# Two slices of the first projection inside the attention prologue: a fused attention and feed-forward kernel on one core, with sums ahead of exps and the fifth unit's loads moved

## The chip, the cores and the metric

The kernel runs on one core of one Trainium2 chip. Time is device time in microseconds (us) of that core, as the median of several runs; one more run is made under the hardware profiler, and from it come the profile page and the trace. TensorE (PE) multiplies matrices and writes to PSUM, VectorE (DVE) and ScalarE (ACT) read PSUM and compute element by element, GpSimd (POOL) computes on SBUF and issues the DMAs that convert types, and SyncE (SP) issues the other DMAs.

## What is computed

```python
q_n = q / (np.linalg.norm(q, axis=-1, keepdims=True) + 1e-06)
k_n = k / (np.linalg.norm(k, axis=-1, keepdims=True) + 1e-06)
scores = np.matmul(q_n, k_n.transpose(0, 1, 3, 2)) / tau
scores = scores - np.max(scores, axis=-1, keepdims=True)
attn = np.exp(scores)
attn = attn / (np.sum(attn, axis=-1, keepdims=True) + 1e-09)
attn_out = np.matmul(attn, v)               # (8, 12, 448, 64)
x = attn_out.transpose(0, 2, 1, 3).reshape(8 * 448, 12 * 64)
h = x @ w_in                                # 768 -> 2048
out = (h * np.cos(h)) @ w_out               # 2048 -> 768
```

There are 8 batches, 12 heads, 448 positions and a head size of 64; tau is 0.1. Inputs and the output are float32 in HBM. With normed q and k no score is large, so the kernel takes exps without subtracting the maximum.

## The kernel before, in words

**Units and pairs.** A unit is six heads of one batch (16 units, `u`); a pair is two heads (48 pairs, `g`, three in each unit, six in each batch). For each unit SP loads q and k as six DMAs of 224 KB (`load`, two for each pair) into `raw`, which has two buffers, so that unit 4 reuses unit 2's buffer pair by pair. POOL loads v and both weight matrices (W1 and W2 in four quarters each) and converts them to bf16.

**Norms.** `square` (ScalarE or POOL) squares q and k, `reduce` (VectorE) sums over the head, `rnorm` (ScalarE, an ln and an exp, marked ln and rn) makes the inverse root, and `scale` (mostly POOL) multiplies: the result is `qks`.

**Transposes.** For pairs 0 to 8 (`g < TD`) TensorE transposes `qks` into a PSUM bank and VectorE copies it to `qkT` (one of three buffers). From pair 9 on SP does it as a DMA transpose (L619, labels T9, T10 ...).

**Attention of a pair.** `scores` runs in four steps c = 0 to 3 (a half one and three full ones), in turn in the PSUM tiles SC1 and SC0; after each, ScalarE takes the exp into `PX` (L666). `attend` multiplies exps by v (marked AV, L690) and by ones for the sums (marked S, L712 or L698), both in the PSUM tile AV; two small opening stages (R, L683) come before. For a direct pair ScalarE then takes lnS and expS (L745, L747), the reciprocal of the sums as exp(-ln), and VectorE multiplies to `xT` (L751; in the first six pairs it reads AV itself, so AV becomes free only then). For the other pairs AV and sums are copied out, and `chain` sends the sums through a gather DMA, a reciprocal, a store to HBM and a broadcast DMA (gather, spread, bcast, all on SP), and POOL multiplies (L784). Unit 2's reciprocal is made on POOL (L770, L771).

**First projection (`m1`).** For each batch, 16 slices n of 128 columns of W1, two slices (n = 2gi and 2gi + 1) in one two-bank PSUM tile; each slice accumulates six matmuls over the six pairs' `xT` (L798, "M1"). ScalarE takes the cosine as a sine (L813), VectorE multiplies (L815) into `gT`. Sine and exp need different ScalarE tables, loaded ahead of and behind `m1` (L498). Before, `m1(0)` takes the tiles SC0, SC1 and AV in turn (`TURN`), and opens its first two gi early, without the last pair.

**Second product (`m2`).** The output is made in 28 tiles of 128 rows. Between other work (`m2_fill`) TensorE takes a tile in quarters of its array (L873, four 64x64 pieces for each of 16 steps y and two halves h) into the banks PO and TP. It is held by the quarter of W2 (`y // 4`) and the slice of `gT` (`y // 2`) that a step reads. Before, tile 0 goes through y = 0 to 15 with h = 0, then with h = 1.

**Order.** All operations go into a `Program` that plays them with written-out costs: on ScalarE, VectorE, POOL and SP the ready operation with the earliest due time (`late`, moved by `bias`) goes next; on TensorE the prologue is chosen from a window of the program's order (`P.free`), and from `P.free = False` on the order is the program's. In TensorE's planned gaps in the prologue `emit` puts filler matmuls of zeros into PO. What an engine does is then fixed; only semaphores set the time. The prologue (L1026 to L1054) is: pairs 0 to 5, the loads of unit 2 and unit 3, weights, the last `attend`, `transposes(6)`, `m1(0)`, and the loads of unit 4 (L1054), which wait for nothing but the buffer. Then come pairs 6 to 47; inside pair 6 the transposes of pairs 7 and 8 stand (L1009 to L1011), the one in TP, the other in PO. `m1(1)` follows after pair 12's scores.

## Time and profile before

| | us |
|---|---|
| median of three runs | 437.56 |
| lowest, highest | 437.56, 440.69 |
| the profiled run | 438.43 |
| its span | 436.6 |
| ScalarE busy | 271.2 |
| POOL busy | 231.0 |

A line of a timeline has the start, the length, the engine, the line of the source, the operation, out <- in, the shape and the count of instructions in the row, and in brackets the idle time of the engine before it with what ended it. A line of the waits has who waited, for whom, the sum in us, how often, and the longest. "DMA to landing" is the smallest, median and largest time from issue to landing of the DMAs that a view chose. The chain is the work that ended last, followed back from the end; its rows have a start, a length and what. TensorE's granted clock is 1.00 all through the profile before.

### The profile page before, as it was taken

How to read it: one execution, taken by the hardware profiler on the slowest of the kernel's cores; microseconds unless marked ns; L12 is line 12 of the kernel's file. 1: busy time of each engine (PE TensorE's matmuls, PEld its weight loads, DVE VectorE, ACT ScalarE, POOL GpSimd, SP SyncE). 2: the span in 40 equal slices, each digit the busy share in tenths (PEclk: the TensorE clock that was granted, in tenths of full speed). 3: DMA queues.
4: the chain of work that ended last, by engine and by line, in shares of the span. 5: the costliest groups of instructions: out<-in, count | busy, mean ns of one | idle time of the engine just before them, and what ended most of it. 6: DMA issues, size and time to landing. Idle time of an engine off the chain costs nothing.

```text
span 436.6 us, 13537 instructions
## 1 busy us (share of the span) xinstructions
PE 419.8 (96%) x6056; PEld 231.5 (53%) x6056; DVE 188.0 (43%) x242; ACT 271.2 (62%) x356; POOL 231.0 (53%) x184
## 2 busy tenths in 40 slices
PE   8889989989999999999999999999999999999996
PEld 4334545545555555564556545665556545455563
DVE  3543762245742348331862158321862144323421
ACT  5987577775787745877478836776478845603400
POOL 4999927669755464744947095905947022003000
PEclk9999999999999999999999999999999999999999
DMA  8999997999669996649927997859956930151022
GB/s 190 250 257 220 245 206 107 164 208 204 125 83 112 214 207 168 137 105 203 238 46 157 181 217 139 137 107 216 235 102 101 149 98 2 40 137 38 2 72 72
DMA packets 80713, 64.32 MB, mean 147 GB/s; under 512 B 45712, under 2 KB 75408, under 8 KB 80656
## 3 DMA queue, kind: packets, MB, share of 16 engines
q1 hardware_dynamic: 62528, 50.68, 56.8%
q0 software_dynamic: 18048, 12.59, 19.5%
q8 instruction: 47, 0.77, 0.8%
q10 hardware_dynamic: 80, 0.20, 0.1%
q14 instruction: 10, 0.08, 0.1%
HBM read 55.67 MB, written 11.14 MB: 153 GB/s over the span
## 4 chain that ended last, share of the span: by engine, by line
PE 56%; DMA 15%; POOL 14%; issue 5%; ACT 3%; SPq 3%; DVE 2%; ACTq 0%; POOLq 0%; DVEq 0%
PE SC L798 16%; PE AV L798 9%; PE TP L873 7%; DMA W<-in_moe_w_out_dram 7%; PE PO L873 7%; POOL qks L602 4%; PE SC L651 4%; PE AV L690 4%; POOL xT L784 4%; POOL sq L570 3%; DMA sums<-xu 3%; DMA RB<-scr 3%; PE PO L903 2%; PE SC L903 2%; PE TP L903 2%
## 5 line engine op out<-in xcount | busy, mean ns | idle before, releaser
L666 ACT ACTIVATE PX<-SC 128x448 bf16<-128x448 f32 (+1 forms) x192 | 153.4, 823 | 27.5 <-PE SC L651 17.0
L873 PE MATMUL PO<-W,gT 64*64 64x384 bf16 x1408 | 143.4, 323 | 1.7 <-DVE qkT L640 0.9
L873 PE MATMUL TP<-W,gT 64*64 64x384 bf16 x1408 | 143.4, 324 | 0.4
L602 POOL TENSOR_TENSOR qks<-raw,rn 128x896 bf16<-128x896 f32 (+1 forms) x48 | 79.4, 1678 | 40.4 <-ACT rn L594 40.4
L798 PE MATMUL SC<-xT,W 128*128 128x448 bf16 x480 | 98.3, 353 | 0.0
L784 POOL TENSOR_TENSOR xT<-xu,RB 128x448 bf16<-128x448 f32 x37 | 41.0, 1136 | 100.7 <-DMA RB<-scr 100.7
L873 PEld LDWEIGHTS PO<-W,gT 64*64 64x64 bf16 x1408 | 76.4, 107 | 19.3 <-issue 3.3
L873 PEld LDWEIGHTS TP<-W,gT 64*64 64x64 bf16 x1408 | 76.1, 107 | 15.8 <-PE TP L873 2.2
L570 POOL TENSOR_TENSOR sq<-raw 128x896 bf16<-128x896 f32 x45 | 75.2, 1693 | 8.4 <-DMA raw<-in_q_dram 6.8
L813 ACT ACTIVATE cosb<-SC,cst 128x896 f32<-128x896 f32 x40 | 40.1, 1006 | 54.6 <-PE SC L798 53.3
L798 PEld LDWEIGHTS SC<-xT,W 128*128 128x128 bf16 x480 | 46.7, 98 | 44.1 <-POOL xT L784 0.4
L798 PE MATMUL AV<-xT,W 128*128 128x448 bf16 x288 | 62.0, 353 | 2.6 <-POOL xT L784 1.4
L577 DVE TENSOR_REDUCE n<-sq 128x14 f32<-128x896 bf16 (+2 forms) x49 | 51.5, 1055 | 6.8 <-ACT sq L568 5.7
L651 PE MATMUL SC<-qkT 64*64 64x448 bf16 x576 | 52.0, 359 | 1.5 <-ACT lnn L591 0.9
L815 DVE TENSOR_TENSOR gT<-SC,cosb 128x896 bf16<-128x896 f32 x40 | 43.5, 1089 | 22.0 <-ACT cosb L813 21.9
L813 ACT ACTIVATE cosb<-AV,cst 128x896 f32<-128x896 f32 x24 | 24.2, 1007 | 39.1 <-PE AV L798 39.1
L846 DVE COPY osb<-PO 128x384 f32<-128x384 f32 x26 | 14.5, 558 | 69.9 <-PE PO L873 63.4
L798 PEld LDWEIGHTS AV<-xT,W 128*128 128x128 bf16 x288 | 26.9, 98 | 32.1 <-POOL xT L784 5.0
L815 DVE TENSOR_TENSOR gT<-AV,cosb 128x896 bf16<-128x896 f32 x24 | 26.2, 1090 | 38.1 <-ACT cosb L813 38.0
L737 DVE COPY xu<-AV 128x896 f32<-128x896 f32 x23 | 25.0, 1086 | 40.5 <-PE AV L706 40.4
L690 PE MATMUL AV<-PX,va 128*32 128x448 bf16 x576 | 36.2, 356 | 0.0
L651 PEld LDWEIGHTS SC<-qkT 64*64 64x64 bf16 x576 | 16.2, 105 | 21.9 <-ACT PX L666 11.1
(66 smaller groups left out, 364.0 us busy)
## 6 DMA issues: line engine op xcount, KB each, us to landing
raw<-in_k_dram SPq DMA_DIRECT2D x48, 224.0 KB, 6.7
raw<-in_q_dram SPq DMA_DIRECT2D x48, 224.0 KB, 7.4
out_dram<-osb SPq DMA_DIRECT2D x55, 192.0 KB, 3.4
RB<-scr SPq DMA_DIRECT2D x22, 336.0 KB, 4.9
va<-in_v_dram POOLq DMA_DIRECT2D x32, 192.0 KB, 9.2
W<-in_moe_w_in_dram POOLq DMA_DIRECT2D x4, 768.0 KB, 15.0
W<-in_moe_w_out_dram POOLq DMA_DIRECT2D x4, 768.0 KB, 26.1
RB<-scr SPq DMA_DIRECT2D x4, 224.0 KB, 4.1
```

The costliest lines, as they stand in the source:

```text
L570: pool(lambda e, x=x, y=y: e.tensor_tensor(y, x, x, ALU.mult), src_, dst, 0.1 + n * 1.78e-3, label="sq%d.%d" % (u, p)).pad = LATE if u > 1 ...
L577: dve(lambda e, w=w: e.tensor_reduce(out=n2v[i][:, 2 * p : 2 * p + 2, w], in_=sqv[p][:, :, w, :], axis=mybir.AxisListType.X, op=ALU.add), ...
L602: f = lambda e, s0=s0, s1=s1: e.tensor_tensor(qksv[i][:, p, s0:s1].rearrange("p s h d -> p h s d"), rawv[i][:, h, s0:s1, :], bass.AP(rn[i] ...
L651: m = e.matmul(SCv[z][BP * o : BP * o + BP, a, 0:S], t[r, c - 1 + (NT3 + 1) * o, 0:BP], t[r, :, BP : 2 * BP], start=True, stop=True)
L666: act(lambda e: e.activation(PHv[j] if c == 0 else PXv[j][:, c - 1], SCv[z][:, :, 0:n], ACT.Exp, scale=1.0 / TAU), ["SC%d" % z], [("PX", j ...
L690: t = e.matmul(AVv[o : o + 32, 0, 0:S], vav[y][:, 2 * p + a, c + 1, d : d + 32], PXv[j][:, c, a, :], start=False, stop=(c == NT3 - 1))
L784: pool(lambda e, p=p: e.tensor_tensor(xTv[b % 2][:, UP * i + p, :], xuv[:, u % 3, p, :], RBv[i][:, p, :], ALU.mult), [("RB", i, p), ("xa", ...
L798: t = e.matmul(ph[:, a, 0:S], W1v[:, order[c], 128 * n : 128 * n + 128], xTv[b % 2][:, order[c], :], start=(c == 0), stop=(c == NKC - 1))
L813: act(lambda e, ph=ph, cz=cz: e.activation(cosv[cz], ph[:, :, 0:S], ACT.Sin, bias=cst.ap()[:, 0:1], scale=1.0), names(gi) + ["cst0"], [("c ...
L815: dve(lambda e, ph=ph, cz=cz, gi=gi: e.tensor_tensor(gTv[:, 2 * gi : 2 * gi + 2, S * (b % 2) : S * (b % 2) + S], ph[:, :, 0:S], cosv[cz], ...
L873: r = e.matmul(POH[b][x : x + 64, 0:HW], gTv[k, y, col + x : col + x + 64], W2v[k, y, HW * b : HW * b + HW], start=(y == 0 and h == 0), st ...
L903: r = e.matmul(po[:, 0:HW], gTv[:, y, col : col + 128], W2v[:, y, HW * hf : HW * hf + HW], start=(y == 0), stop=(y == NF - 1))
```

## The change

PO and TP become the two halves of one two-bank PSUM tile MP, so MP can hold two slices of the first projection. Its parts:

- The slices n = 0 and 1 of `m1(0)` accumulate the first four pairs' `xT` in MP right behind pair 5's last scores (`m1_step`, called in the prologue), then pair 4's and pair 5's. The order of tiles in `m1(0)` becomes MP, SC0, SC1, AV, twice (`first`), with three gi opened early. The number of matmuls is the same.
- The transposes of pairs 6, 7 and 8 stand inside `m1(0)`, at gi = 5, 6 and 7 (`inner`), all three in TP. Before, one stood ahead of it and two behind it.
- lnS and expS of the first six pairs are due 1.0 earlier (`bs`).
- Fillers stop at the last opening of the two slices, and after the first opening they add zeros without clearing the bank. The program has 50 in place of 61.
- Unit 4's loads of q and k wait until slice gi = 6 of `gT` is written (`u4`), which is inside `m1(0)`.
- Tile 0 of the second product goes through y = 0 to 7 for both halves, then y = 8 to 15 (`cut`).

What this does to the order on the engines: on TensorE nine matmuls of the first projection stand ahead of pair 5's last sum, before it was five; from the first matmul of the second product on, TensorE's order is the same. On ScalarE lnS and expS go ahead of the second half of the next pair's exps, and after `m1(0)` unit 3's ln comes behind five exps and its rn behind six (before, behind two), unit 4's much later. On VectorE the second copy of pair 0's transposes goes ahead of a reduction. On POOL a square and a W1 issue go ahead of the third scale, ahead of the sixth stand one square and one W1 issue more than before; after `m1(0)` unit 4's squares come between unit 3's second and third scale. On SP unit 4's loads stand just ahead of T9, unit 5's are split around T11, and the store of unit 2's reciprocals is followed by an output, T12 and the broadcast.

The diff, cut to its core:

```diff
     "late": 0.0,
     "mixed": (3, (0, 1, 2, 0, 1, 2, 0, 1), (2, 3, 4, 0, 1, 5)),
-    "other": 8,
-    "inside": 7,
+    "turned": 9,
+    "first": (3, 1, 2, 0, 3, 1, 2, 0),
+    "inner": 5,
+    "bs": -1.0,
+    "cut": 8,
+    "bx": 0.0,
...
+    "u4": (6,),
+    "v3": (),
...
+            opened = [o.start for o in self.ops if o.label == "M1 0.0"]
             for a, b in self.gaps:
                 t, a = a + room / 2, a + room
-                while a + took <= b:
-                    o = self.op("PE", fn, cost=took, mode="F", label="filler")
+                while a + took <= min(b, max(opened)):
+                    o = self.op("PE", lambda e, shut=t < min(opened): fn(e, shut), cost=took, mode="F", label="filler")
...
-    TPF = ps("TP", [128, 512], F32)
-    TP = TPF.bitcast(BF16)
-    AVT = AV.bitcast(BF16)
-    PO = ps("PO", [128, 512], F32)
-    POT = PO.bitcast(BF16)
+    MP = ps("MP", [128, 2 * 512], F32)
+    TPF, PO = MP.ap()[:, 0:512], MP.ap()[:, 512:1024]
+    TP, AVT = MP.bitcast(BF16).ap()[:, 0:1024], AV.bitcast(BF16).ap()
...
-        if g == PLAN["other"]:
-            bank, keys = [POT, POT], [["PO"], ["PO"]]
...
         act(lambda e: e.activation(xuv[:, 3 + i, p, :], AVv[:, 1, 0:S], ACT.Ln), ["AVs"], [("xs", i, p)], S, "E",
-            label="lnS%d" % g)
+            label="lnS%d" % g, bias=PLAN["bs"] if g < PB else 0.0)
         act(lambda e: e.activation(r, xuv[:, 3 + i, p, :], ACT.Exp, scale=-1.0), [("xs", i, p)], [("RB", i, p)], S, "E",
-            label="expS%d" % g)
+            label="expS%d" % g, bias=PLAN["bs"] if g < PB else 0.0)
...
+    BANKS = {"AV": ["AVa", "AVs"], "MP": ["TP", "PO"]}
+
+    def m1_step(b, bank, n, c0, c1, order):
+        a, (name, ph) = n % 2, PHs[bank]
+
+        def f(e):
+            for c in range(c0, c1):
+                t = e.matmul(ph[:, a, 0:S], W1v[:, order[c], 128 * n : 128 * n + 128], xTv[b % 2][:, order[c], :],
+                             start=(c == 0), stop=(c == NKC - 1))
+            return t
+
+        return P.op("PE", f, [("W1", n // 4)] + [("xT", b % 2, order[c]) for c in range(c0, c1)], BANKS.get(name, [name]),
+             cost=(c1 - c0) * MM, mode="F", label="M1 %d.%d" % (b, n))
+
+    def m1(b, early=0, split=NKC, turn=TURN, order=tuple(range(NKC)), done=0, inner={}):
...
+        for gi in range(done):
+            for a in range(2):
+                step(gi, a, NKC - 2, NKC - 1)
         for c0, c1 in [(0, split)] + [(c, c + 1) for c in range(split, NKC - 1)]:
-            for gi in range(early):
+            for gi in range(done, early):
                 for a in range(2):
                     step(gi, a, c0, c1)
         for gi in range(NF // 2):
+            if gi in inner:
+                transposes(inner[gi])
...
-        h, y0 = f // NF, f % NF
+        seg = [(h, y, w) for y, w in ([(0, PLAN["cut"]), (PLAN["cut"], NF - PLAN["cut"])] if t == 0 else [(0, NF)]) for h in range(2)]
+        at = f
+        while at >= seg[0][2]:
+            at -= seg.pop(0)[2]
+        h, y0 = seg[0][0], seg[0][1] + at
...
-    P.filler = (lambda e: e.matmul(PO.ap()[:, 0:S], zt.ap()[:, 0:128], zt.ap(), start=True, stop=True), zero, MM, 0.3)
+    P.filler = (lambda e, shut: e.matmul(PO[:, 0:S], zt.ap()[:, 0:128], zt.ap(), start=shut, stop=shut), zero, MM, 0.3)
...
         if g == PB:
-            for y in range(PLAN["inside"], TD):
-                transposes(y)
             m2_fill(f[1], True)
...
     for g in range(PB):
         pair(g, (0, 0, 0, 0))
+        if g == PB - 1:
+            for a in range(2):
+                P.order_only(find("SC%d.3" % g), m1_step(0, 3, a, 0, PB - 2, tuple(range(NKC))))
...
-    for g in range(PB, PLAN["inside"]):
+    for g in range(TD, LT):
         transposes(g)
-    m1(0, 2, NKC - 1)
-    load_v(3, find("W2.3"))
+    m1(0, 3, NKC - 1, PLAN["first"], done=1, inner={PLAN["inner"] + g - PB: g for g in range(PB, TD)})
+    load_v(3, find("W2.3"), [("gT", 0, x) for x in PLAN["v3"]])
     norms(3, 1)
     load_v(4, find("load v u3"))
-    loads(4)
+    loads(4, None, [("gT", 0, x) for x in PLAN["u4"]])
```

More of the change, by code (lines that the diff above doesn't have):

```diff
@@ L534, in load @@
             behind = P.ops[-1] if x == (1,) else behind
-            dma(eng, [f[y] for y in x], (), [("raw", i, p, y) for p in range(p0, p1) for y in x] + (["first"] if (u, p0) == (0, 0) and 1 in x else []),
+            dma(eng, [f[y] for y in x], list(reads), [("raw", i, p, y) for p in range(p0, p1) for y in x] + (["first"] if (u, p0) == (0, 0) and 1 in x else []),
                 "raw%d_%d_%s" % (i, p0, x), 0.97 * (p1 - p0) * len(x), "load u%d p%d" % (u, p0), behind, 1.8,
@@ L625, in half @@
             for s in range(s0, s1):
-                r = e.transpose(bank.ap()[:, 128 * s : 128 * s + 128], qksv[i][:, p, s], ident.ap())
+                r = e.transpose(bank[:, 128 * s : 128 * s + 128], qksv[i][:, p, s], ident.ap())
             return r
@@ L958, in direct, with loads @@
         return g in PLAN["direct"]
-    def loads(u, behind=None):
+    def loads(u, behind=None, reads=()):
         if u < NU:
             for p in range(UP):
-                load(u, p, p + 1, behind=behind)
+                load(u, p, p + 1, behind=behind, reads=reads)
     def m2_at():
@@ L1016, in pair @@
             transposes(g + 1, g + 1 < PLAN["apart"])
-        if TD <= g + 2 < NG:
+        if max(TD, PB + 2) <= g + 2 < NG and g + 2 >= LT:
             transposes(g + 2)
@@ L1074, in bass_cosine_attention__then__act_gcu_kernel @@
     m2_add(B - 1)
[L1075 removed]
+    banks[0] = [(["PO"], PO), (["TP"], TPF)] + [(BANKS.get(n, [n]), x[:, 0, :]) for n, x in PHs[:3]]
     m2_fill(10 ** 6)
```

37 lines of the change are left out of this document (14 added, 23 removed).

## The prediction

> **What bounds it now.** I read the page's first lines, then who waited for whom on TensorE (from 59 to 75 us), then a table of stretches that I cut at the starts of stages, then the engines' rows in order of time.
>
> ```profile
> span 436.6 us, 13537 instructions
> PE 419.8 (96%) x6056; PEld 231.5 (53%) x6056; DVE 188.0 (43%) x242; ACT 271.2 (62%) x356; POOL 231.0 (53%) x184
> ```
> ```profile
> PE PO L873 <- DVE qkT L640: 0.9, 1, 0.9
> PE PO L873 <- DMA W<-in_moe_w_out_dram: 0.8, 1, 0.8
> ```
> ```profile
> 11.75:39.10 27.35, 24.07 (x325) 10.47 (x326) 12.36 (x17) 24.73 (x44) 26.60 (x22) 1.00 1.20 246
> 41.84:59.42 17.58, 17.48 (x95) 8.75 (x91) 13.37 (x14) 9.35 (x10) 12.43 (x10) 1.00 1.17 237
> 66.24:92.54 26.30, 26.15 (x608) 15.65 (x597) 8.67 (x13) 20.26 (x29) 18.63 (x13) 1.00 0.89 145
> ```
>
> In the table the columns are the stretch, its length, busy time of PE, PEld, DVE, ACT and POOL, the granted clock, the DMA share and GB/s. TensorE is full from the first projection (41.84) to the second (92.54), except for the two waits above: what comes earlier at its start comes earlier behind it. Before 39.1 TensorE is not the bound, since its busy time there holds zero-filler matmuls; ScalarE works 24.73 of 27.35 us (mostly the exps of the six prologue pairs), POOL 26.60. The span belongs to a run of 438.43 us, 0.87 above the median of 437.56; I subtract from both alike.
>
> **Part 1: sums ahead of exps, and the slices.** Rows of ScalarE, VectorE, TensorE and POOL around the first and the last prologue pairs:
>
> ```profile
> 11.46 0.31 ACT L591 ACTIVATE lnn<-n,cst 128x14 f32<-128x14 f32 x1 [0.71 <-DVE n L577]
> 11.80 0.22 ACT L594 ACTIVATE rn<-lnn 128x14 f32<-128x14 f32 x1
> 12.09 6.23 ACT L666 ACTIVATE PX<-SC 128x448 bf16<-128x448 f32 x8
> ```
> ```profile
> 37.71 0.58 ACT L747 ACTIVATE RB<-xu 128x448 f32<-128x448 f32 x1
> 38.18 0.92 ACT L666 ACTIVATE PX<-SC 128x896 bf16<-128x896 f32 x1
> ```
> ```profile
> 10.35 1.08 DVE L577 TENSOR_REDUCE n<-sq 128x14 f32<-128x896 bf16 x1
> 11.35 0.35 DVE L640 COPY qkT<-AV 128x384 bf16<-128x384 bf16 x1
> ```
> ```profile
> 38.33 0.62 DVE L751 TENSOR_TENSOR xT<-AV,RB 128x448 bf16<-128x448 f32 x1 [2.87 <-ACT RB L747]
> ```
> ```profile
> 40.59 0.75 PE L690 MATMUL AV<-PX,va 128*32 128x448 bf16 x12
> 41.17 0.74 PE L712 MATMUL AV<-PX,ones 128*32 128x448 bf16 x12
> 41.84 3.77 PE L798 MATMUL SC<-xT,W 128*128 128x448 bf16 x19
> ```
> ```profile
> 24.96 1.69 POOL L602 TENSOR_TENSOR qks<-raw,rn 128x896 bf16<-128x896 f32 x1
> ```
>
> The order of the changed program puts the AV copy ahead of the 1.08 us reduction, so the first exp starts at about 11.45 instead of 12.09, while one ln/rn pair (0.31 + 0.22) moves in behind it. ScalarE's work until its last prologue exp ends (now 39.10) is then about 25.2 us. With no idle time that is 36.6; with today's (27.35 - 24.73 = 2.6) it is 39.2. Walking the new order pair by pair with these durations (eight exps of two pairs take 6.23), ScalarE waits 0.5 each for the sums of the first and the third pair and little else: I take 37.6, a gain of 1.5. What the sums cost the exps is hidden, since the next scores need banks that those exps free and TensorE's fillers, not work, stand there; without that slack each sum would cost about 1 us.
>
> After the last exp, 2.74 us pass today until the last sum ends at 41.84. The expS of the fifth pair (37.71) stands between the two exps, its product is done at 38.95, then come the last pair's opening matmuls and five matmuls of the first projection, and AV at 40.59. In the new order expS goes ahead of both exps, the product is done near 36.7, nine projection matmuls stand around it while ScalarE still works, and AV and the sums (0.58 + 0.67) end about 1.0 after the last exp. Gain 1.7. Last sum: 41.84 - 1.5 - 1.7 = 38.6. The slices themselves bring only nine matmuls there in place of five; that is counted next. POOL scales q and k of the sixth pair 2.5 later than now (24.96), because one more square and one more W1 issue go ahead, and ends at 29.1; the transposes are due at 30.7, so it costs nothing, but with 1.6 less it would push the last pair.
>
> **Part 2: the first projection with the transposes inside.** One row is the chain's, for the price of a matmul (24 in 4.54); the others are TensorE's.
>
> ```profile
> 103.59 4.54 PE SC L798 x24
> ```
> ```profile
> 59.84 0.56 PE L626 MATMUL TP<-ident,qks 128*128 128x128 bf16 x7
> 60.24 0.55 PE L626 MATMUL PO<-ident,qks 128*128 128x128 bf16 x7
> 61.74 0.32 PE L873 MATMUL PO<-W,gT 64*64 64x384 bf16 x1 [0.95 <-DVE qkT L640]
> ```
>
> A matmul costs 0.189, seven transposes 0.40. From the last sum to the first matmul of M2 (the second product) it is 61.74 - 41.84 = 19.9 now. After: 96 - 9 = 87 matmuls, 16.45; three sets of transposes, 1.2; some 0.3 before the third set, because all three use one bank now and VectorE does a slice's product before the copy; two scores, 0.4; the rest of the last copy, 0.5: 18.85. Gain 1.05, and M2 starts at 57.45. The table load back to exps then ends some 0.8 behind M2's start, so scores wait 0.6 for exps; but the ln/rn pairs that stand between those exps now move behind them, and the 0.78 wait for W2 falls away at that place (part 3). The scores that come at 66.24 now, 4.5 after M2's start, come about 3.95 after it: gain 0.55. Sum there, if no load is late: 1.5 + 1.7 + 1.05 + 0.55 = 4.8.
>
> **Part 3: the loads.** The chain's row for W2, a step of M2, the transposes on SP, and POOL's queue in ten us with the fifth unit's loads beside it (42 to 52) and in ten without (53 to 63):
>
> ```profile
> 35.18 30.67 DMA W<-in_moe_w_out_dram
> ```
> ```profile
> 68.79 0.32 PE L873 MATMUL TP<-W,gT 64*64 64x384 bf16 x1
> ```
> ```profile
> 65.61 4.96 SPq L619 DMA_TRANSPOSE qkT<-qks  x2
> ```
> ```profile
> q0 software_dynamic: 1189, 1.20, 70.9%
> ```
> ```profile
> q0 software_dynamic: 1510, 2.06, 116.1%
> ```
>
> The last quarter of W2 lands at 65.85. Without the fifth unit POOL's queue moves 2.06 in place of 1.20 MB in 10 us, and would be 0.86/0.206 = 4.2 earlier, 61.7. But the loads come back when slice 6 of gT is done, 17 us behind the last sum, at 55.65, and flow from about 58; W2's last 0.75 MB then go at 0.12 MB/us and land near 64.3. Cutting tile 0 at 8 needs that quarter eight steps later, where M2 stands at 68.79 now: 64.0 after. Cost 0.3, between 0 and 1.
>
> The larger cost is on SP. The DMA transposes of pair 9 are issued at 65.61 today, into an empty hardware queue. After, they are issued at about 64.9 (unit 3's ln/rn comes behind the exps, POOL's scale behind that), and the six loads are ahead of them. The fifth unit's six loads today; six later ones; then the time to landing of pair 9's transposes, and of the small store issued 0.65 behind the later six; then pair 9's first scores:
>
> ```profile
> L530 SPq DMA_DIRECT2D raw<-in_k_dram x3: 595/595/605, 38.4 to 41.7; - x3
> L530 SPq DMA_DIRECT2D raw<-in_q_dram x3: 607/607/1010, 39.0 to 42.3; - x3
> ```
> ```profile
> DMA to landing us min/median/max: 5.9/8.2/10.3
> ```
> ```profile
> L530 SPq DMA_DIRECT2D raw<-in_k_dram x3: 611/612/644, 79.1 to 81.8; - x3
> L530 SPq DMA_DIRECT2D raw<-in_q_dram x3: 607/607/630, 79.8 to 82.4; - x3
> ```
> ```profile
> DMA to landing us min/median/max: 3.4/4.1/5.5
> ```
> ```profile
> DMA to landing us min/median/max: 5.3/5.3/5.3
> ```
> ```profile
> DMA to landing us min/median/max: 5.0/5.0/5.0
> ```
> ```profile
> 74.79 0.27 PE L659 MATMUL SC<-qkT 64*64 64x224 bf16 x4
> ```
>
> The six took from 38.4 to 42.3 + 10.3 = 52.6, 14.2 us beside POOL's queue; the later six 82.4 + 5.5 - 79.1 = 8.8 alone. So the fifth unit ends between 64.5 and 69.9. The transposes end between 67.6 (2.7 after issue) and 71.9 (2 behind the last load). Pair 9's scores, at 74.79 now, would come at 70.3 (4.8 - 0.3 earlier): a wait of 0 to 1.6. POOL's queue still holds W2 and v then, so the upper row is nearer; I take 0.9. Left at pair 9: 4.8 - 0.3 - 0.9 = 3.6.
>
> [...]
>
> **Part 4: the second projection's wait.** TensorE's waits from 92 to 99, and the chain:
>
> ```profile
> PE AV L798 <- POOL xT L784: 1.1, 2, 1.0
> PE AV L798 <- POOL xT L751: 0.2, 1, 0.2
> ```
> ```profile
> 94.76 2.21 POOL xT L784 x2
> ```
>
> It starts at 92.54 and waits 1.27 for products on POOL that hang on the broadcast of unit 2's reciprocals. The gather, the store and the broadcast move forward by about 4, and SP has one transpose ahead of the broadcast in place of two: it lands at 87 to 89 instead of 94.7. TensorE needs the first product at 92.54 - 3.6 + 12 x 0.189 = 91.2, POOL, with scales, squares and two other products ahead, ends it between 89 and 91. I take 1.2 of 1.27; with POOL 1.5 later nothing is won.
>
> Sum: 3.6 + 1.2 = 4.8. 438.43 - 4.8 = 433.6 for a profiled run, 432.8 on the median. Behind that TensorE's order is the same, and I cost the rest at nothing: the same waits, moved.
>
> **Rivals.**
> - Nothing waits: the loads go as those at 79.1 did. 4.8 + 1.27: 431.5. For it: the hardware queue is otherwise empty. Against it: POOL's is not.
> - The load only moves the wait: pair 9's transposes take their own 5.3 behind the loads and end near 74.6. Pair 9 gains about 0.2, the projection 1.2: 436.2. For it: the DMA share is 1.17 until 59.42, so what moves meets other traffic. [...]
> - Slower: POOL in its new order does the fifth unit's squares ahead of unit 2's reciprocals and products. If those loads land late, pair 12's scale and the second projection follow, one us for one. It decides some 5 us behind my 69.9, and 9 us behind gives 442. Against it: six such loads took at most 14.2.
> - The sums' place does nothing: ScalarE keeps its 2.6 of idle time, the last exp ends at 39.2, and the gain falls by 1.6: 434.4.
>
> **Chances.** As summed 0.52, own range 431.5 to 434.2; nothing waits 0.13; wait moved 0.16; idle kept 0.10; slower 0.09. A measurement of this kernel tells about 1% (4.4 us, so 433.2) from no change. Two thirds of the first and all of the second case lie below that: faster 0.47. The rest but the slow case: same 0.43. Slower 0.10, with a tail of the third. The range, 431.2 to 436.5, leaves out the slow case and the ends of the second and third.
>
> **What would show it.** Right: the last prologue sum at 38 to 39.2; M2 from 57 to 58; pair 9's scores at 70 to 72, behind a short wait for a DMA; under 0.5 of waiting in the second projection. Wrong: the last prologue exp at 39 or later, a wait over 1 for W2, pair 9 past 73, or POOL's squares waiting over 3 for the fifth unit.

## The result, and the profile after

The changed kernel's median is 436.94 us (435.3 to 438.21, 12 runs). In the same comparison the kernel before stands at 439.93 (12 runs), above the 437.56 of its first three runs. The ratio is 0.9943, with a 95% interval of 0.9922 to 0.9964: 2.5 us won (1.6 to 3.4), where 4.8 were forecast. Worked from the ratio alone, 437.56 x 0.9943 = 435.1. The ratio and its interval rest on fast runs alone; of the kernel before's twelve, one (447.94) is a slow one. The profiled run took 435.3, 3.1 less than the one before, and it is the fastest of the twelve.

The first lines of the page after, and the table of stretches, cut at the same places as before (first exp, last exp; last sum, pair 6; pair 7's second scores, second projection), but that the first row before began 0.34 ahead of its first exp:

```profile
span 433.5 us, 13510 instructions
PE 417.8 (96%) x6045; PEld 230.9 (53%) x6045; DVE 188.3 (43%) x242; ACT 270.6 (62%) x356; POOL 230.6 (53%) x184
```
```profile
11.43:39.14 27.71, 24.41 (x323) 10.31 (x319) 12.98 (x17) 24.43 (x43) 27.33 (x22) 1.00 1.20 247
40.40:58.46 18.06, 17.91 (x112) 9.60 (x109) 12.12 (x13) 9.88 (x11) 8.79 (x8) 1.00 1.20 208
63.25:90.13 26.88, 26.56 (x600) 15.52 (x601) 12.17 (x17) 21.19 (x34) 22.57 (x15) 1.00 0.86 190
```

In the first row ScalarE works 24.43 of 27.71 us: it begins 0.66 earlier than before and ends where it ended (39.14 against 39.10). From the first exp to the last its idle time grew from 2.5 (24.50 of 27.01 us busy) to 3.3. ScalarE's, POOL's and TensorE's rows show where:

```profile
11.43 1.35 ACT L669 ACTIVATE PX<-SC 128x448 bf16<-128x448 f32 x2 [0.61 <-PE SC L662]
12.67 0.31 ACT L596 ACTIVATE lnn<-n,cst 128x14 f32<-128x14 f32 x1
...
14.81 0.21 ACT L599 ACTIVATE rn<-lnn 128x14 f32<-128x14 f32 x1
...
19.68 0.54 ACT L748 ACTIVATE xu<-AV 128x448 f32<-128x448 f32 x1 [1.44 <-PE AV L715]
```
```profile
12.94 1.71 POOL L575 TENSOR_TENSOR sq<-raw 128x896 bf16<-128x896 f32 x1
14.56 0.90 POOL L935 DMA_DIRECT2D W<-in_moe_w_in_dram  x1
15.47 1.70 POOL L607 TENSOR_TENSOR qks<-raw,rn 128x896 bf16<-128x896 f32 x1
```
```profile
17.23 0.56 PE L631 MATMUL MP<-ident,qks 128*128 128x128 bf16 x7 [0.47 <-POOL qks L607]
17.73 0.28 PE L686 MATMUL AV<-PX,va 64*64 64x224 bf16 x2
...
18.89 0.74 PE L715 MATMUL AV<-PX,ones 128*32 128x448 bf16 x12
```

Before, the first value product, the first sum and its lnS were:

```profile
16.97 0.26 PE L683 MATMUL AV<-PX,va 64*64 64x224 bf16 x1
...
18.11 0.74 PE L712 MATMUL AV<-PX,ones 128*32 128x448 bf16 x12
```
```profile
18.90 0.54 ACT L745 ACTIVATE xu<-AV 128x448 f32<-128x448 f32 x1
```

Read from below: the first sum (TensorE, 18.89) ends 0.8 later than before, behind the first value product at 17.73; that stands behind the third pair's transposes, which wait for POOL's third scale; and that comes behind a square and a W1 issue, since the third pair's rn now ends at 15.02, not 12.02. Something else that the first value product needs comes at the same moment, the first V load, two DMAs issued at 5.9 and 6.7:

```profile
L549 POOL DMA_DIRECT2D va<-in_v_dram x2: 667/752/836, 5.9 to 6.7; - x2
DMA to landing us min/median/max: 7.9/9.1/10.3
```

The later one lands at 6.72 + 10.35 = 17.07, 0.1 before the scale ends. Behind the prologue, the start of M2, pair 9's and pair 12's first scores, and TensorE's waits from 59 to 75:

```profile
59.34 0.36 PE L890 MATMUL MP<-W,gT 64*64 64x384 bf16 x4 [0.40 <-DVE qkT L643]
```
```profile
72.09 0.27 PE L662 MATMUL SC<-qkT 64*64 64x224 bf16 x4
```
```profile
86.84 0.29 PE L662 MATMUL SC<-qkT 64*64 64x224 bf16 x4
```
```profile
PE SC L654 <- ACT PX L669: 0.4, 1, 0.4
PE MP L890 <- DVE qkT L643: 0.4, 1, 0.4
```

M2 starts 2.40 earlier, the wait for W2 is gone, and there is none for a DMA at pair 9.

### The profile page after: what moved, and what is told of

It reads as the page before. It is cut to its first block, busy times and chain, and to the rows that moved or that the text cites. A ratio compares the mean times of both kernels' runs of the same rounds, so it can differ in the third digit from the quotient of the medians.

```text
span 433.5 us, 13510 instructions
## 1 busy us (share of the span) xinstructions
PE 417.8 (96%) x6045; PEld 230.9 (53%) x6045; DVE 188.3 (43%) x242; ACT 270.6 (62%) x356; POOL 230.6 (53%) x184
## 4 chain that ended last, share of the span: by engine, by line
PE 68%; POOL 9%; ACT 6%; DMA 6%; issue 4%; SPq 3%; DVE 3%; ACTq 0%; POOLq 0%; DVEq 0%
PE SC L797 18%; PE MP L890 17%; PE AV L797 10%; PE AV L693 5%; PE SC L654 5%; PE MP L920 4%; POOL qks L607 4%; POOL xT L787 4%; ACT PX L669 2%; DMA RB<-scr 2%; PE AV L686 2%; PE SC L920 2%; ACT cosb L826 2%; DVE gT L828 1%; PE AV L701 1%
## 5 line engine op out<-in xcount | busy, mean ns | idle before, releaser
L890 PE MATMUL MP<-W,gT 64*64 64x384 bf16 x2816 | 144.9, 324 | 1.2 <-DVE qkT L643 0.4
L890 PEld LDWEIGHTS MP<-W,gT 64*64 64x64 bf16 x2816 | 79.0, 107 | 34.4 <-issue 4.2
L797 PE MATMUL SC<-xT,W 128*128 128x448 bf16 x468 | 96.0, 352 | 0.0
L826 ACT ACTIVATE cosb<-SC,cst 128x896 f32<-128x896 f32 x39 | 39.2, 1006 | 53.0 <-PE SC L797 49.8
L797 PE MATMUL AV<-xT,W 128*128 128x448 bf16 x276 | 59.7, 353 | 2.6 <-POOL xT L787 1.6
L859 DVE COPY osb<-MP 128x384 f32<-128x384 f32 x50 | 25.9, 552 | 72.3 <-PE MP L890 61.7
L828 DVE TENSOR_TENSOR gT<-SC,cosb 128x896 bf16<-128x896 f32 x39 | 42.5, 1089 | 23.6 <-ACT cosb L826 23.3
L826 ACT ACTIVATE cosb<-AV,cst 128x896 f32<-128x896 f32 x23 | 23.2, 1007 | 37.6 <-PE AV L797 36.0
L797 PEld LDWEIGHTS AV<-xT,W 128*128 128x128 bf16 x276 | 25.8, 98 | 30.6 <-POOL xT L787 5.2
L828 DVE TENSOR_TENSOR gT<-AV,cosb 128x896 bf16<-128x896 f32 x23 | 25.1, 1090 | 37.9 <-ACT cosb L826 37.8
L686 PE MATMUL AV<-PX,va 64*64 64x224 bf16 x192 | 25.7, 260 | 1.3 <-ACT PX L669 1.0
L686 PE MATMUL AV<-PX,ones 64*64 64x224 bf16 x192 | 25.7, 260 | 0.0
```

Of the source, the lines that this page charges most:

```text
L686: m = e.matmul(AVq[64 * a : 64 * a + 64, k, :, o, :], w, PHv[j][r, a, :], start=(n == 0), stop=False)
L797: t = e.matmul(ph[:, a, 0:S], W1v[:, order[c], 128 * n : 128 * n + 128], xTv[b % 2][:, order[c], :], start=(c == 0), stop=(c == NKC - 1))
L826: act(lambda e, ph=ph, cz=cz: e.activation(cosv[cz], ph[:, :, 0:S], ACT.Sin, bias=cst.ap()[:, 0:1], scale=1.0), names(gi) + ["cst0"], [("c ...
L828: dve(lambda e, ph=ph, cz=cz, gi=gi: e.tensor_tensor(gTv[:, 2 * gi : 2 * gi + 2, S * (b % 2) : S * (b % 2) + S], ph[:, :, 0:S], cosv[cz], ...
L890: r = e.matmul(POH[b][x : x + 64, 0:HW], gTv[k, y, col + x : col + x + 64], W2v[k, y, HW * b : HW * b + HW], start=(y == 0 and h == 0), st ...
```

## The experiments

My theory from the two traces (A): the last exp stayed at 39.1 because the third pair's norm comes late. Against it stood that the sums' new place makes ScalarE wait (B), that V's landing holds the first sum (V), and that a stage behind takes up whatever the prologue wins (C). All runs in one table: where lnS of the first and of the sixth pair starts on ScalarE, where M2, pair 9's and pair 12's first scores start on TensorE, and where the last instruction ends (3.1 before the span's end), each from the profiled run; then the ratio of the times to the kernel before's, measured on the same chip.

| kernel | first lnS | sixth lnS | M2 | pair 9 | pair 12 | last | ratio, 95% |
|---|---|---|---|---|---|---|---|
| before | 18.90 | 41.96 | 61.74 | 74.79 | 89.28 | 433.6 | |
| after | 19.68 | 40.52 | 59.34 | 72.09 | 86.84 | 430.4 | 0.9943 (0.9922-0.9964) |
| c_after | 19.23 | 40.07 | 58.89 | 71.87 | 87.65 | 433.1 | 0.9955 (0.9923-0.9988) |
| e_bs0 | 19.26 | 41.42 | 60.25 | 73.00 | 87.49 | 431.9 | 0.9975 (0.9945-1.0005) |
| b_bs | 18.75 | 40.88 | 61.05 | 73.41 | 87.90 | 432.5 | 0.9972 (0.9948-0.9996) |
| e_noslice | 19.27 | 40.80 | 60.38 | 73.13 | 87.61 | 431.3 | 0.9954 (0.9928-0.9981) |
| e_u4early | 19.54 | 40.37 | 59.43 | 71.95 | 86.75 | 432.1 | 0.9946 (0.9918-0.9974) |
| e_rn | 18.86 | 40.23 | 59.05 | 71.81 | 86.29 | 431.3 | 0.9951 (0.9922-0.9981) |
| e_nov | 16.07 | 38.08 | 56.90 | 70.42 | 84.93 | 429.2 | a single run, 434.46 (before 438.10) |
| e_rnnov | 16.39 | 37.66 | 56.48 | 70.43 | 84.94 | 429.0 | a single run, 433.95 (before 438.10) |
| e_vearly | 17.80 | 39.89 | 58.72 | 71.47 | 89.88 | 433.9 | 1.0026 (0.9995-1.0057) |
| e_vsplit | 16.04 | 38.05 | 56.87 | 72.59 | 87.10 | 430.4 | 0.9979 (0.9946-1.0012) |
| e_vsplitrn | 16.79 | 38.62 | 57.44 | 72.58 | 87.08 | 433.5 | 0.9950 (0.9915-0.9986) |
| e_vsplitu4 | 16.30 | 38.30 | 57.37 | 75.86 | 91.27 | 436.5 | 1.0030 (0.9998-1.0063) |
| e_vsplitw8 | 15.99 | 40.02 | 58.84 | 71.59 | 88.19 | 432.0 | 0.9909 (0.9883-0.9936) |
| e_vsplitw4 | 17.06 | 39.39 | 58.21 | 71.85 | 86.71 | 430.7 | 0.9943 (0.9923-0.9962) |
| e_vsplitw12 | 16.19 | 50.51 | 69.33 | 82.09 | 96.57 | 438.3 | 1.0119 (1.0091-1.0147) |

`c_after` is the changed kernel once more, and from the first lnS to M2 its profile stands 0.45 ahead of the first one: a difference of that size between two profiles tells nothing. The time from the first lnS to the sixth, 20.84, is the same in both.

**1. The sums' place.** `e_bs0` is the changed kernel, `b_bs` the kernel before, each with one number changed:

```diff
-    "bs": -1.0,
+    "bs": 0.0,
```
```diff
-            label="lnS%d" % g)
+            label="lnS%d" % g, bias=-1.0 if g < PB else 0.0)
```

(the same for expS). Expected of `e_bs0`:

> The changed kernel with the sums' logarithms and reciprocals in the prologue back at their old places in ScalarE's order (the slices and the later loads stay). Theory A (the last prologue exp stayed at 39.1 because the third pair's norm comes 3.0 us later, so ScalarE stands idle 1.44 before the first sum; the sums' place is not what cost it): the idle before the first sum stays above 1, the last exp ends at 38.5 to 39.3, the fifth pair's expS stands between the last two exps again, and M2 starts 0.7 to 1.5 later than the changed kernel's 59.34; the whole is 0.5 to 1.5 us slower than the changed kernel. Rival B (the sums ahead of the exps keep ScalarE waiting): the last exp ends at 38.0 or earlier, and M2 starts at or before 59.3. Rival C (what the prologue gains or loses is taken up at the fourth first projection, where POOL's products wait for a broadcast): the prologue moves by up to 1.5 and the end by under 0.4.

Without the earlier sums the last exp ends 1.1 earlier (38.05), below the range that I gave, and M2 starts 0.91 later, as I gave. Rival B had the first all but right and the second wrong. ScalarE's rows of `e_bs0` there:

```profile
36.70 0.54 ACT L748 ACTIVATE xu<-AV 128x448 f32<-128x448 f32 x1
37.14 0.91 ACT L669 ACTIVATE PX<-SC 128x896 bf16<-128x896 f32 x1
37.94 0.58 ACT L750 ACTIVATE RB<-xu 128x448 f32<-128x448 f32 x1
41.42 0.55 ACT L748 ACTIVATE xu<-AV 128x448 f32<-128x448 f32 x1 [2.91 <-PE AV L715]
```

The exps run ahead, expS (37.94) stands behind the last of them (I gave: between the last two), and ScalarE then idles 2.91. So the last exp's end is no measure of the prologue; the last sum is.

> The kernel before with only the sums' logarithms and reciprocals of the prologue put ahead of the exps. By V2 the first sum stays near 18.9, the later ones follow by about 4.2 in place of 4.6, and the last one's logarithm starts at 39.5 to 40.6 in place of 41.96; M2 starts 1.4 to 2.4 before 61.74; the end is 0.5 to 1.5 earlier than before, since the W2 wait at 66 (0.78, where it lands at 65.85) and the W2 and q/k loads in POOL's and SP's queues stay where they are. If the slices or the later loads are what brings the gain, the last sum's logarithm stays within 0.4 of 41.96 and the time within 0.5 of the kernel before.

Alone on the kernel before, the earlier sums bring 1.08 at the sixth lnS (40.88, 0.3 past the range), 0.69 at M2 (I gave 1.4 to 2.4) and 0.28% of the time. From the first to the sixth lnS there are five steps; one step takes (41.96 - 18.90)/5 = 4.61 before, 4.43 in both of these, 4.17 in both profiles of the changed kernel. The rival, that the sums' place does nothing, falls.

**2. What holds the first sum.** `e_rn` puts the third pair's ln and rn ahead of the exps on ScalarE, `e_nov` lets the first pair's value products read zeros and so wait for no V, `e_rnnov` does both:

```diff
                 rnorm(u, p, p + 1, z)
+                if x == 2:
+                    find("ln0.2").bias = find("rn0.2").bias = -8.0
```
```diff
+                w = zt.ap()[:, 0:32] if g == 0 else vav[y][:, 2 * p + a, c + 1, d : d + 32]
...
-[("va", y), ("PX", j, c + 1)]
+["zt" if g == 0 else ("va", y), ("PX", j, c + 1)]
```

(the same for the opening stages).

> The changed kernel with the third pair's ln and rn put right behind its reduction on ScalarE, ahead of the exps. Theory A: rn ends near 13.2 in place of 15.02, POOL's third scale ends near 15 to 16.4 in place of 17.17, the idle before the first sum falls from 1.44 to under 0.7, the last exp ends at 37.9 to 38.6, and the whole is 0.5 to 1.2 us faster than the changed kernel. Rival V (the first value products wait for the first V load, which landed at 17.07, so that nothing ahead of it moves them): the first value product starts at 17.2 or later, the first sum's logarithm at 19.1 to 19.7, the last exp stays within 0.3 of 39.1, and the time within 0.4 of the changed kernel's. Rival C: the last exp at 38.6 or earlier, but the end within 0.4 of the changed kernel's.

> The changed kernel with the first pair's value products taken over a tile of zeros instead of V (the first pair's result is left out, so that TensorE need not wait for the first V load there); the third pair's norm is as late as in the changed kernel. Rival V: the first sum's logarithm comes at 17 or earlier, and the last exp ends 0.8 or more before 39.14. Theory A: the first sum comes early, but the second pair's last exps are followed by an idle of 1 us or more all the same, because the third pair's scores wait for the late scale (its scale ends at about 17.2); the last exp ends at 38.3 to 39.2.

> Both together: the third pair's norm early, and the first pair's value products over zeros (the first pair's result is left out). If V's landing and the late norm each hold up ScalarE by about the same moment (both near 17.1), only this one lets ScalarE run on: no idle over 0.4 before the third pair's exps and the last exp at 36.8 to 37.8. By theory A alone it ends where the kernel with the early norm alone ends; by rival V alone, where the one over zeros alone ends.

The early norm takes the idle 1.44 away and brings the first lnS 0.82 forward, but the sixth only 0.29, and against `c_after` not at all: theory A falls, its idle time moves to the next sum. Zeros in place of V bring the first lnS to 16.07, the sixth to 38.08 and M2 to 56.90, a little earlier than the forecast's prologue (last sum 38.6, M2 57.45). Both together bring 0.42 more. Rival V holds, with one correction. In `e_rn` V landed at 15.03, yet the first value product came at 16.62: it stands behind all the second pair's scores in TensorE's order, which was planned with V's load in it. Without V in the plan it stands at 11.88. And with the changed kernel's order there, an earlier V does nothing: it landed at 15.47 in `e_bs0` and at 15.24 in `e_u4early`, and their first lnS came at 19.26 and 19.54, since TensorE still waited for POOL's scale ahead of the third pair's transposes. TensorE's waits of `e_u4early` from 13 to 19:

```profile
PE MP L631 <- POOL qks L607: 1.0, 2, 0.5
```

So it is the order built on V's load that holds the first sum; an earlier V pays only with an order that counts on it.

ScalarE, VectorE and TensorE in `e_rn` show why a later norm or exp matters little once the first sum is set:

```profile
18.86 0.52 ACT L748 ACTIVATE xu<-AV 128x448 f32<-128x448 f32 x1
19.42 0.58 ACT L750 ACTIVATE RB<-xu 128x448 f32<-128x448 f32 x1
```
```profile
20.17 0.62 DVE L754 TENSOR_TENSOR xT<-AV,RB 128x448 bf16<-128x448 f32 x1
```
```profile
20.93 0.28 PE L686 MATMUL AV<-PX,va 64*64 64x224 bf16 x2 [0.59 <-DVE xT L754]
...
22.28 0.74 PE L715 MATMUL AV<-PX,ones 128*32 128x448 bf16 x12
```

The product reads the bank AV, so the next pair's first matmul waits for it; sum, lnS, expS, product, opening, values, sum take 4.21 from 18.86 to the next lnS at 23.07. It is a loop through one bank, and six pairs go through it. Work moved on ScalarE beside it did not shorten it (a step takes 4.27 here, 4.17 in the changed kernel); what moves the last sum is when the loop begins. Not all of an earlier beginning arrives: of 3.61 us at the first lnS of `e_nov` 2.44 are left at the sixth, since one step takes 4.40 there; why is not shown.

**3. V earlier, in a kernel that computes everything.** `e_vearly` issues the first V load first of all; `e_vsplit` cuts it, the first pair's two heads at the old place and the other four behind the first scale:

```diff
-    load_v(0, None, first)
+    load_v(0, None, ())
```
```diff
-    load_v(0, None, first)
+    load_v(0, None, first, 0, 2)
     first = [("qks", 0, 0, 0)]
+    load_v(0, None, first, 2, UH)
...
```

(the heads are new arguments of `load_v`, and each pair's products wait for their own heads).

> The changed kernel, correct, with the first unit's V load issued at the start of POOL's queue, not behind the landing of the first q and k. Theory V2 (formed after the runs with zeros: the first pair's value products wait for the first V load, at 17.07 in the changed kernel, the first sum follows it by about 2, and each later sum follows the one before by 4.15 to 4.4, so the place of the first sum sets that of the last one): V lands at 10 to 14, the first sum's logarithm starts at 16.0 to 17.5 in place of 19.68, the last one's at 37.5 to 38.8 in place of 40.52, M2 starts at 56.5 to 58.0 in place of 59.34. Theory C2 (behind M2's start, part of it goes to pair 9's wait for the fifth unit's loads and to the fourth first projection's wait for POOL's products): pair 9's scores at 70 to 71, and the end 0.8 to 2 us earlier than the changed kernel's, less than the 1.5 to 2.8 of M2's start. Rival: the V load takes its bandwidth from the first q and k, the first exp comes 1 us or more later than 11.43, and M2 starts within 0.5 of the changed kernel's.

> The changed kernel, correct, with the first unit's V load cut in two: the first pair's two heads where the whole load stood, the other four heads behind the first scale on POOL. By V2: the first pair's V lands at 9 to 12 in place of 17.07 and the first exp stays at 11.1 to 11.9; the first sum's logarithm starts at 16 to 17.3, the last one's at 37.5 to 38.7, M2 starts at 56.6 to 57.9 in place of 59.34; pair 9's scores then wait 0.3 to 1 for their transposes, as with the zeros, at 70.4 to 71; pair 12 comes at 84.9 to 85.8 in place of 86.84, and the end 1.0 to 2.0 us earlier than the changed kernel's. Rival: the V load is bound by its packets, not by its bytes ahead of it, lands at 13 or later, and M2 starts at 58.5 or later; or W1's quarters, which POOL now issues later, are waited for at the first projection.

`e_vearly` is half V2 and half the rival: V lands at 8.48, but the first exp comes 1.4 later (12.82), M2 wins only 0.62, and pair 12 then waits 3.7 for its transposes. `e_vsplit` meets the forecast of the prologue (first lnS 16.04, sixth 38.05, M2 56.87) but for V itself, which lands at 12.46 where I gave 9 to 12; and it wins nothing in time. TensorE's waits from 56 to 75 say what took it back:

```profile
PE MP L890 <- DMA W<-in_moe_w_out_dram: 1.8, 1, 1.8
PE SC L662 <- DMA qkT<-qks: 0.8, 1, 0.8
```

POOL now issues W1's first two quarters at 22.7 and 23.5, not at 10.4 and 14.6, so what stands behind them in its queue is late; W2's last quarter is issued at 43.15, not at 35.88, and lands at 65.30 in place of 60.74. I had looked for that wait at the first projection.

**4. What takes it back.** The unedited kernel again, and two more with the cut load:

> The changed kernel once more, unedited, so that the next three stand beside it on the same chip. If the fourth first projection takes up what the prologue brings (theory C), its waits for POOL's products of over 1 us are there again, and pair 12's first scores to the end takes 0.5 us or more above the kernel before's 344.27. If those waits are scatter, the places and sizes of the waits behind pair 12 differ from the first profile's, while pair 12 to the end again takes 343.6 to 345.4, as in the ten profiles so far, whatever the prologue did in them.

> The cut V load and the third pair's norm ahead of the exps together. With the zeros the norm brought 0.42 at M2's start (56.90 to 56.48) and nothing at pair 12 (84.93 to 84.94), since pair 9 waits for its transposes: M2 starts 0 to 0.6 before the kernel with the cut V load alone, pair 12 and the time are the same within 0.4.

> The cut V load with the fifth unit's q and k loaded early, as in the kernel before. Pair 9 then no longer waits behind those loads, but W2's last quarter lands at 64 to 65, and M2, which starts at 56.6 to 57.9, needs it near 64: a wait of 0.3 to 1.3 there and none at pair 9. If the later loads pay only when M2 starts early (they brought nothing at 59.4), pair 12 comes 0 to 0.8 later than with the cut V load and the later loads, and the second first projection waits 0.5 more.

`c_after` waits 1.0 for pair 12's transposes, 2.5 with no releaser shown, and 1.4 for POOL's products in pieces of at most 0.6. The first profile had 0, 0.4 and 1.6, with 1.2 of it at one place:

```profile
PE MP L890 <- issue: 1.6, 1, 1.6
PE AV L797 <- POOL xT L787: 1.4, 6, 0.6
PE SC L662 <- DMA qkT<-qks: 1.0, 1, 1.0
PE AV L693 <- issue: 0.9, 1, 0.9
```

So theory C falls as a fixed toll, though the stretch behind pair 12 (345.4) is as long here as I gave it for C. From pair 12 to the last instruction all seventeen profiles take 343.3 to 346.5, but for the 341.7 of `e_vsplitw12`, and early pair 12s are followed by no more than late ones (`e_nov` 344.3 behind 84.93, the kernel before 344.3 behind 89.28); what is not waited for at one place is at another. That scatter of 3 us in one profile is as large as the gain, and only the medians can tell the kernels apart there. `e_vsplitrn` starts M2 0.57 later than `e_vsplit` (its first exp came 0.37 later), not earlier, and pair 12 is the same, 87.08, as given. `e_vsplitu4` is worse than I gave: W2's last quarter lands at 68.00, M2 waits 4.2 for W2, TensorE runs 3.4 us at half its clock behind that (last section), and the time is the slowest but one.

Three more put W1's first quarters back, at three places (bias 8, 4 and 12):

```diff
     load_w1(1, None, first)
+    find("W1.0").bias = find("W1.1").bias = -8.0
```

> The cut V load, with the first two quarters of W1 issued early on POOL again (one behind the rest of the first unit's V, one behind the second unit's first scale), where the plain cut let POOL push them from 10 and 14 us to 22.7 and 23.5. If the weights' queue took back the 2.47 us (W2's last quarter landed at 65.30 there, in place of 60.74): W2's last quarter lands at 60 to 62, M2 starts at 56.6 to 57.9 and does not wait for W2; pair 9's scores come at 70.0 to 71, pair 12 at 84.8 to 86.0, and the time is 0.8 to 2.0 us below the changed kernel's (ratio to the kernel before 0.990 to 0.994). If it is the fifth unit's q and k that take it back, pair 9's scores come at 72 or later, behind a DMA wait of 1 or more, though W2 is early, and the time is the changed kernel's.

> The same with W1's first quarter behind the second unit's second square, about 5 us later than in the one with the greater bias: W2's last quarter lands between 61 and 64, and what M2 waits for it (0 to 1) is what pair 9 and pair 12 come later than there, if the weights' queue is the cause; the same within 0.4 if it isn't.

> The same with W1's first quarter even ahead of the rest of the first unit's V, and the second unit's V behind: the weights land earliest, W2's last quarter at 59 to 61.5; but the second and third pairs' V lands 1 to 4 later than with the plain cut (15.77 and 17.58 there), so that the second sum (20.74 there) comes at 20.7 to 23, and M2 starts 0 to 2 later. If V is what holds the sums, this one starts M2 later than the one with the lesser bias; if nothing waits for V any more, at the same time.

With 8, W2 lands at 59.70 and no step of M2 waits for it, as the weights' theory has it; but the second unit's V now lands at 28.81, the fourth pair's lnS waits until 32.01, and M2 starts at 58.84. Pair 12 waits 1.9 for its transposes, and the half clock comes behind that too. I gave M2 at 56.6 to 57.9 and pair 12 at 84.8 to 86.0, and both were missed. Yet its median, 434.82, has the lowest ratio of all, 0.9909, which I did give: by luck, as far as the profile shows. Its interval overlaps the changed kernel's, and its one profile, taken of the slowest of its twelve runs, does not show what won. With 4, W2 lands at 63.21, no step of M2 waits for it, and pair 9 waits 0.42 for its transposes: M2 58.21 and the changed kernel's time. With 12 the rest of the first unit's V comes behind W1, at 23.5 and 26.3, and the second sum waits for it; TensorE, and ScalarE's second lnS:

```profile
26.30 0.40 PE L686 MATMUL AV<-PX,va 64*64 64x224 bf16 x2 [3.13 <-DMA va<-in_v_dram]
```
```profile
29.68 0.54 ACT L748 ACTIVATE xu<-AV 128x448 f32<-128x448 f32 x1 [1.37 <-PE AV L715]
```

The second sum comes 9 us later than in `e_vsplit` (I gave 0 to 2.3), the sixth 12 later, the time 1.2% above the kernel before. So V and the weights share one queue on POOL, and in these runs each place that one won the other lost: this, more than the fifth unit's loads (0.8 of 2.6 in `e_vsplit`), took back what the cut load won.

**5. The other parts of the change.** `e_noslice` drops the two slices' accumulation in the prologue (their matmuls move behind the last product), `e_u4early` the wait of unit 4's loads:

```diff
-        if g == PB - 1:
-            for a in range(2):
-                P.order_only(find("SC%d.3" % g), m1_step(0, 3, a, 0, PB - 2, tuple(range(NKC))))
...
-    m1(0, 3, NKC - 1, PLAN["first"], done=1, inner=...)
+    m1(0, 3, NKC - 1, PLAN["first"], done=0, inner=...)
```
```diff
-    "u4": (6,),
+    "u4": (),
```

> The changed kernel without the two slices' early accumulation in the prologue (their matmuls stand behind the last product; sums first, later loads and the inner transposes stay). The prediction's price for the slices is four matmuls of 0.189: M2 starts 0.6 to 1.0 later than the changed kernel's 59.34 and the last sum's end moves by under 0.4. Rival (the slices stand in the last sums' way or the fillers' place costs as much): M2's start moves by under 0.3.

> The changed kernel with the fifth unit's q and k loaded as early as in the kernel before (the wait for slice 6 of the first gT dropped). If the later loads are what saves the wait for W2: the last quarter of W2 lands at 64 to 66 in place of 60.74, M2's steps wait 0.5 to 1.5 for it, and pair 9's scores come 0.5 to 1.5 later than 72.09. Rival (the later loads buy nothing that lasts: M2 catches up by pair 12 or by the fourth first projection): the whole is within 0.5 us of the changed kernel's, though pair 9 moves.

The slices bring 1.04 at M2 and 0.28 at the last sum against the first profile, a little more than priced; against `c_after`, whose first lnS is nearer (19.23 to 19.27), they bring 1.49 and 0.73. The later loads bring nothing at this start of M2: W2's last quarter lands at 64.40 in `e_u4early`, as given, but M2 does not wait, because tile 0, cut at 8, needs it later than that, at 65.67; uncut, it would need it at about 62.5, where the 49th of M2's matmuls stands. Pair 9 comes at 71.95 and the ratio is the same. The rival holds. With M2 at 57 they matter: `e_vsplitu4` against `e_vsplit`.

In time none of these parts can be told from the whole change: the intervals of `e_bs0`, `b_bs`, `e_noslice` and `e_u4early` overlap the changed kernel's. What a part is worth is read from single profiles.

## Why the prediction was right and wrong

**The step that failed** is Part 1's walk: "ScalarE waits 0.5 each for the sums of the first and the third pair and little else: I take 37.6, a gain of 1.5." It lets ScalarE's whole list move up with the first exp. The first sum did not move with it: it came 0.78 later, behind the third pair's late scale, in an order that was built on V's load. ScalarE waited 1.44, 0.40 and 0.50 for the first three sums, and its last exp ended at 39.14. Neither V's landing nor the order that hangs on it was a term of the sum, though V stands in the trace of before 0.13 ahead of the first value product. `e_nov` and `e_vsplit` show the rest of Part 1: with V out of the way the last exp ends at 36.7 (37.6 forecast) and the last sum at 38.0 (38.6 forecast).

Step by step, forecast against the profile after:

| step | forecast | measured |
|---|---|---|
| last prologue exp | 1.5 | -0.04 |
| from there to the last sum | 1.7 | 1.48 |
| last sum to M2 | 1.05 | 0.96 |
| M2 to the scores of pair 7 | 0.55 | 0.59 |
| W2 and the cut | -0.3 | -0.29, none of it a wait for W2 |
| pair 9 | -0.9 | 0 |
| second projection | 1.2 | 0.91 |
| behind it | 0 | -0.5 |
| sum | 4.8 | 3.1 |

The 0.9 that pair 9 did not cost hides a part of the miss; it did not cost it because M2 came late.

- Part 1, second half: right. expS goes ahead of the exps, and the last sum ends 1.26 behind the last exp (1.0 forecast, 2.74 before).
- Part 2: right, to 0.1 in both steps.
- Part 3, W2: it landed at 60.74, as "without the fifth unit" would have it (61.7), not near 64.3. That M2 came late is not the reason: in `e_nov` the six loads came back at 54.97, and W2 still landed at 61.77, so the 0.12 MB/us forecast for its last part did not come. That the step measured -0.29 is luck. From pair 7 to pair 8 the gain falls from 2.99 to 2.70 without a wait for W2; tile 0 changes its bank half there once more than before, which would explain it, but no run took the cut alone.
- Part 3, pair 9: the wait is real, but its condition was missed by 1.9 us: the transposes landed at 70.17, the scores came at 72.09. In `e_nov`, where M2 starts at 56.90, pair 9's scores come at 70.42 and lose 0.76 against the changed kernel (0.9 forecast); 0.41 of it is the wait for their transposes (1.0 in `e_rnnov`), the rest a stop of M2 ahead of them for which the trace shows no releaser. The transposes (the first of three) landed 0.95 behind the last of the six loads there; times of issue, and from issue to landing, of both:

```profile
L624 SPq DMA_TRANSPOSE qkT<-qks x3: 1248/1343/2187, 64.2 to 72.4; - x3
...
DMA to landing us min/median/max: 2.6/5.3/6.2
```
```profile
L535 SPq DMA_DIRECT2D raw<-in_q_dram x3: 607/607/607, 55.6 to 58.2; - x3
...
DMA to landing us min/median/max: 6.4/7.9/11.2
```

The transposes issued at 64.18 are the 6.2, and land at 70.38; the last load, issued at 58.20, is the 11.2, and lands at 69.43. In the thirteen profiles with the later loads pair 9's landed 0.65 to 4.0 behind the last of the six, never ahead; that they land 2 behind it at the latest was the forecast's estimate. But the six are not all that they can wait for: in `e_vsplitu4`, where the six had landed at 53.76, those issued at 61.71 took 9.5 us, while W2 was still coming in on POOL's queue (until 68.00). How the wait divides between the two queues no run here shows.
- Part 4: the 1.27 fell to 0.25; the gain from pair 9 to the projection's end is 0.91.
- Behind it: "the same waits, moved" held to half a microsecond in this profile. In the others the time from pair 12 to the last instruction was up to 0.9 less (2.5 in `e_vsplitw12`) and up to 2.2 more than the 344.27 before.
- Rivals: "the sums' place does nothing" gave the last exp at 39.2, where it came, but for another reason: `e_bs0` and `b_bs` show that the sums' place brings 0.7 to 0.9 at M2. Its price, a gain of 3.2, is nearest the 2.5 measured; that too is luck. (As a time the 436.94 is nearer to the rival with the moved wait, 436.2.) The slow rival did not come: the fifth unit's loads landed at 69.50. Pair 12's transposes landed 0.04 before their scores all the same, and in `c_after` and `e_vsplitw8` pair 12 waited 1.0 and 1.9 for them; but they were issued no later there (81.87 and 83.26, against 83.33) and took 5.7 and 4.9 us to land in place of 3.5, which is not that rival's way.
- The range was too narrow at the top by 0.4 us; in that comparison the kernel before stood 2.4 us higher than when the range was made, and the 435.1 worked from the ratio lies inside.

Left open: the price of the cut, of the transposes inside `m1(0)` and of the fillers, none of which had a run of its own; why steps take 4.40 when the first sum comes early; and what makes `e_vsplitw8` the fastest, since its profiled run is the slowest of its twelve.

## What to carry to other kernels

Before you shift a whole list of work forward with its first item, look for each input in it that comes from outside, and write its landing, and the order that was planned around it, into the sum: here one V load, 0.13 us ahead of its first user. Where a loop runs through one buffer, the time of its last turn is the start of the first plus the turns (4.2 to 4.6 us here), and work moved beside the loop mostly moved idle time (in `e_rn` 0.82 us came forward at the first sum, 0.29 at the sixth). A load pulled forward in a shared queue pushed another one back here (W2's last quarter, to 65.30 from 60.74); follow the one that is pushed until its user.

## What the runs showed of the hardware

In four of the seventeen profiles TensorE ran at half its clock, each time for 3.41 us: behind a pause in its matmuls of 3.13 us in `e_vsplitw12`, 3.75 in `e_vearly`, 3.03 in `e_vsplitu4` and 1.94 in `e_vsplitw8`. In `e_vsplitw12` the granted clock (the third column from the right) goes to 0.50:

```profile
23.00:26.30 3.30, 0.17 (x4) 0.00 (x0) 1.08 (x1) 0.00 (x0) 1.72 (x2) 0.98 1.24 221
26.30:29.30 3.00, 3.00 (x36) 1.12 (x36) 0.00 (x0) 0.95 (x3) 0.92 (x1) 0.50 1.19 263
```

The clock fell at 26.17, 91.27, 67.98 and 89.63; in `e_vearly` and `e_vsplitw8` that was 1.4 us after the matmuls had begun again. The first record of 1.00 stands at 5.69, 5.93, 6.54 and 4.29, and each fall came a whole number of steps of 3.41 us behind it (6, 25, 18 and 25). Ahead of that record a 128x448 matmul takes 0.58 us in place of 0.35, in the profile before too (until 7.54), although the view reads 1.00 there. The step that ended with the fall held 3.12, 2.03, 2.97 and 1.94 us without a matmul, so 1.94 of its 3.41 us were enough in `e_vsplitw8`; behind a pause of 1.82 in `e_vsplit` (63.52 to 65.34) it did not fall: the next twelve 128x448 matmuls over V, at 68.35, took 0.75 us there, and 1.25 at the fall in `e_vsplitw8`. At half the clock a 64x384 matmul of `e_vsplitu4` took 0.52 us in place of 0.32.

The first V load, uncut and at its old place, landed between 15.03 and 17.07 in ten profiles. In the same ten pair 12's transposes took 3.5 to 6.3 us from issue to landing.
